# A spectral block with a feed-forward layer: memory laid out anew, a second output set, weight parts dealt out anew, and another order of asking in the planner

## The chip, the cores and the metric

The kernel runs on one core of one Trainium2 chip. The metric is the device time of one execution in microseconds (us); the profiler's views come from one profiled execution of the same program. The engines are TensorE (PE in the views; PEld is its weight load), VectorE (DVE), ScalarE (ACT), GpSimd (POOL) and SyncE (SP), whose queue issues most of the DMAs.

## The reference

One layer of 4096 tokens of 640 features in float32. The shift, scale and gate vectors come from a small modulation product `silu(c) @ w_mod`.

```python
def _A_ref(x, w1, b1, w2, b2):                 # 4096 tokens, NB = 4 blocks of 160 features
    z = rfft over the tokens, split into the 4 blocks -> zr, zi
    hr = relu(zr @ w1[0] - zi @ w1[1] + b1[0]);  hi = relu(zi @ w1[0] + zr @ w1[1] + b1[1])
    or_ = hr @ w2[0] - hi @ w2[1] + b2[0];       oi_ = hi @ w2[0] + hr @ w2[1] + b2[1]
    or_, oi_ = soft shrinkage of both by 0.01
    return irfft(or_ + 1j * oi_)

def _B_ref(x, w_gate, w_up, w_down):
    return (silu(x @ w_gate) * (x @ w_up)) @ w_down     # 640 -> 1728 -> 640

h = layernorm(x) * (1 + ca) + sa
x = x + ga * _A_ref(h, ...)
h = layernorm(x) * (1 + cb) + sb
x = x + gb * _B_ref(h, ...)
return x
```

## The kernel before

A product keeps float32's accuracy by parts: each operand is rounded to a high part of a shorter float32 form (`F32R`), and the rest is its low part; a product is then high by high, high by low and low by high. So every weight and every activation passes two steps before a matmul may read it: a "high" (a copy or a scaling, on ACT or POOL) and a "low" (a subtract, on VectorE or POOL).

**First half (the spectral part).** The token index is split in 128 by 32 for the Fourier transform. Eight tiles `xa0` to `xa7` of x (each 10,240 bytes of a partition) are normalized and transformed; `write_s1` copies each result to the device memory `s1` in several pieces. The frequencies are then worked in eight chunks `ch` of four blocks `b`, in a loop over positions `p = 4 ch + b` whose order is written out by hand (`manual_schedule`): each engine works its instructions in the order in which they stand in the code. At position p stand, in this order: layer one of block p (`stage_l1`, tiles `pl`, `h`, `u`, `r2`); the second transform for later blocks (`stage_b`, tile `pb`; `evac_b` reads it into the parts `z`, ACT first, then VectorE); `tail_low` of block p; layer two of block p - 1 (`stage_l2`, tile `pc`; two groups of eight matmuls, each followed by a VectorE addition of the bias into `tts`, called `tt`); the inverse transform of a block some positions back (`stage_i`, tile `pi`). After the last block of a chunk, `move_x` copies the chunk's two `tt` tiles by eight DMAs into other tiles, `xx`. The tag `tt` has two buffers, so the next chunk's first addition waits until these copies have landed.

Layer two's weights are three pairs: `w2a`, `w2b` and `w2c`, each of 640 features in two halves o = 0 and 1. `prep2` lists the six jobs in the order w2a 0, w2a 1, w2b 0, w2b 1, w2c 0, w2c 1. The kernel before gives POOL the highs of jobs 0, 2 and 5 and the low of 5; ACT has the highs 1, 3 and 4, and VectorE the lows 0 to 4 (0 and 1 ahead of the loop, 2 to 4 at its first position).

The tiles of layer two and of the inverse (pool `p2`) lie in the memory of the `xa` tiles, which is free again when the last copies of a tile have been read. With `reuse_waits="tile"` an instruction that first writes such a tile waits for those older tiles only that lie in the same place. From the addresses: before, `acc`, `cl`, `wx` and `bx` lie in xa0, `w2a` in xa1, `w2b` in xa2, `w2c` in xa3 and the `tt` set in xa4.

**Second half (the feed-forward part).** From about 311 us on, 32 rows of 128 tokens are worked in six tiles, the first two (`plain`) by straight products, the other four (`seven`, `down7`) by seven products of half size for eight. Its order is worked out when the program is built: a planner holds chains of steps, each with an engine, an assumed duration and what it depends on, and keeps an assumed time of each engine. After every stretch of matmuls (`slot`, by 0.3 us) it calls `sweep`, which asks each chain in turn for the steps that may be issued by now. `tails` are short chains that follow a product (the parts of an activation, its products and differences); then come the standing chains, first `gate` (the gate's sum) and `prep` (highs and lows of the gate and up weights, line 1413 on ACT and line 1420 on VectorE). Which step is asked first is issued first on its engine.

Of the kernel before, what the change touches and what calls it, by code (L numbers as in the profile page):

```python
# [6 lines left out]
F32 = mybir.dt.float32  # L7
F32R = mybir.dt.float32r
AF = mybir.ActivationFunctionType
OP = mybir.AluOpType  # L10
# [3 lines left out]
P = 128  # L14
D = 640
# [3 lines left out]
NB = 4  # L19
# [154 lines left out]
def body(tc, x, w1, b1, w2, b2, wg, wu, wd, c, wm, k_fa, k_tb, k_tx, k_bm, k_bx, k_ga, k_ge, k_id, out, dbg=None):  # L174
# [4 lines left out]
    def f32(ap):  # L179
        return ap.bitcast(F32)  # L180
# [21 lines left out]
    with ExitStack() as top:  # L202
# [35 lines left out]
        with ExitStack() as af:  # L238
# [40 lines left out]
            def weights_high(w, h, l, v, sg, eng=None):  # L279
                if eng:  # L280
                    eng.tensor_scalar(w[:, :, h], v, sg, None, op0=OP.mult)
                else:
                    act.activation(w[:, :, h], v, AF.Copy if isinstance(sg, float) else AF.Identity, scale=sg)

            def weights_low(w, h, l, v, sg):
                dve.scalar_tensor_tensor(w[:, :, l], v, sg, f32(w[:, :, h]), op0=OP.mult, op1=OP.subtract)
# [52 lines left out]
            b2t = rp.tile([P, 2, NB, BS], F32, name="b2t")  # L339
            with tc.tile_pool(name="sp", bufs=1) as sp:  # L340
                xas = []

                def load_x(t):
                    xa = xp.tile([P, 4, D], F32, name=f"xa{t}")
                    if t < 3:
                        for i in range(4):
                            nc.sync.dma_start(xa[:, i, :], xv[:, 4 * t + i, :])
                    else:
                        nc.sync.dma_start(xa, xv[:, 4 * t:4 * t + 4, :])
                    xas.append(xa)  # L350
# [156 lines left out]
            nc.sync.dma_start(tx, k_tx)  # L507
            p2 = af.enter_context(tc.tile_pool(name="p2", bufs=1, side="right", reuse_waits="tile"))

            acc = p2.tile([P, D], F32, name="acc")  # L510
            cl = p2.tile([P, D], F32, name="cl")
            wx = p2.tile([P, P], F32, name="wx")
            bx = p2.tile([P, 2, 128], F32, name="bx")
            w2a = p2.tile([P, NB, 640], F32R, name="w2a")
            w2b = p2.tile([P, NB, 640], F32R, name="w2b")
            w2c = p2.tile([P, NB, 640], F32R, name="w2c")
            prep2 = prep_weights(raws[2], w2a, w2b, w2c, False)

            prep2 = [prep2[i] for i in (0, 3, 1, 4, 2, 5)]
            for n in (0, 2, 5):  # L520
                weights_high(*prep2[n], pool)
            w, h, l, v, _ = prep2[5]
            pool.tensor_tensor(w[:, :, l], v, f32(w[:, :, h]), op=OP.subtract)


            nc.sync.dma_start(bx.rearrange("p a b -> p (a b)"), k_bx)
# [55 lines left out]
            pbs = {}  # L582
            rzs = {}
            hss = {}
            tts = {}

            def width(ch):
                return 258 if ch == CE else 256
# [1 line left out]
            def stage_b(ch, t, tag=None):  # L590
                g, tb = gs[ch], tbs[ch]
                pb = (ps.tile([P, 2, 256], F32, tag=tag, name=f"pb{ch}_{t}") if tag else
                      bank0(1 if t == 4 else 0, [P, 2, 256], f"pb{ch}_{t}"))
                col = slice(128 * t, 128 * t + 128)
                for j in range(4):
                    mm(pb[:, :, 64 * j:64 * j + 64], g[:, j, col], tb[:, j, :], start=True, stop=True)
                pbs[ch, t] = pb
# [90 lines left out]
                                         op0=OP.max, op1=OP.subtract)  # L688


            def stage_l2(ch, b, then=()):
                h0, h1, r2, _ = hss[ch, b]
                de = slice(160 * b, 160 * b + 160)
                for q in ((0, 2, 1) if ch == CE else (0, 1)):
                    fs = slice(128 * q, 128 * q + 128) if q < 2 else slice(256, 258)
                    M = 128 if q < 2 else 2
                    W = 320 if q < 2 else 160
                    if b == 0 and q < 2:
                        tts[ch, q] = p2.tile([P, 2, D], F32, tag="tt", bufs=2, name=f"tt{ch}_{q}")
                    pc = ps.tile([P, 512], F32, tag="p2" if q < 2 else "p1", name=f"pc{ch}_{b}_{q}")  # L700
                    seq = [(h0[:, 0, fs], w2a[:, b, 0:W]), (h0[:, 1, fs], w2a[:, b, 0:W]),
                           (h0[:, 0, fs], w2a[:, b, 320:320 + W]),
                           (h1[:, 0, fs], w2b[:, b, 0:W]), (h1[:, 1, fs], w2b[:, b, 0:W]),
                           (h1[:, 0, fs], w2b[:, b, 320:320 + W]),
                           (r2[:, fs], w2c[:, b, 0:W]), (r2[:, fs], w2c[:, b, 320:320 + W])]
                    for i, (l, m) in enumerate(seq):
                        mm(pc[:M, :W], l, m, start=(i == 0), stop=(i == len(seq) - 1))  # L707
                    if q < 2:
                        dve.tensor_tensor(tts[ch, q][:, :, de], pc[:, :320].rearrange("p (r e) -> p r e", r=2),
                                          b2t[:, :, b, :], op=OP.add)  # L710
                        if then:
                            then[q]()
                    else:

                        dve.tensor_tensor(tts[ch, 0][0:1, 1, de], pc[0:1, :160], b2t[0:1, 0, b, :], op=OP.add)
# [52 lines left out]
            e32 = hp.tile([P, 5, 2], F32, name="e32")  # L768
            edge = hp.tile([P, 2, 5, 2, 2], F32R, name="edge")
            zero = hp.tile([P, 2, 5, 2, 2], F32, name="zero")  # L770
            pool.memset(zero, 0.0)
            pool.tensor_copy(edge, zero)


            def edges():
                px = ps.tile([P, 5, 2], F32, tag="p3", name="px")
# [13 lines left out]
                evac_b(0, b)  # L790
                evac_r(0, b)
            weights_high(*prep2[1])
            for job in prep2[0:2]:
                weights_low(*job)


            def shrink_last(q, hf):
# [28 lines left out]
            for p in range(LAST + 1):  # L826
                ch, b = p // 4, p % 4
                on(shrink, p - 6)
                on(stage_l1, p)


                if p < 4:
                    todo = ([(0, 2)], [(0, 3)], [(1, 4), (1, 0)], [(1, 1)])[p]
                elif b == 0:
                    todo = [(ch, 3)]
                else:
                    todo = [(ch + 1, 4)] * (b == 1) + [(ch + 1, b - 1)]
                todo = [q for q in todo if q[0] < NCH]
                for q in todo:
                    stage_b(*q)  # L840
                    if q[1] < 4:
                        evac_b(*q)
                for f, *a in sums.get(p, ()):
                    f(*a)

                rows = [p + 2] * (p < 4) + [p + 3] * (p > 2)
                for k in rows:
                    on(evac_rh, k)
                on(tail_l1, p)
                on(shrink_high, p - 6)  # L850
                for k in rows:
                    on(evac_rl, k)
                on(tail_low, p)
                on(stage_l2, p - 1)
                if p == 3:
                    stage_b(1, 2)
                    evac_b(1, 2)
                on(stage_i, p - 7)
                on(shrink_low, p - 6)
                if p < LAST:  # L860
                    on(shrink_parts, p - 5)
                if b == 0 and ch:
                    for i in range(4):
                        move_x(ch - 1, i)
                if p == 0:
                    for n in (3, 4):
                        weights_high(*prep2[n])
                    for job in prep2[2:5]:
                        weights_low(*job)
                if p == 0:  # L870
                    pool.dma_start(bm.rearrange("p a b c -> p (a b c)"), k_bm)
                if p == 2 or b == 3 and 2 < ch + 2 < NCH:
                    load_g(ch + 2)
                    load_tb(ch + 2)
                for f, *a in mods.get(p, ()):
                    f(*a)
                if p == LAST - 4:
                    cf += [rp.tile([P, 2, D], F32, tag=tag, name=f"cf{tag}") for tag in ("rm", "rr")]
                    load_first_rows(rb + 16, rl, nc.sync)
                elif p == LAST - 1:  # L880
                    load_first_rows(0, rb - 16, nc.sync)
# [163 lines left out]
        with ExitStack() as ff:  # L1045
# [76 lines left out]
            class Chain:  # L1122
# [4 lines left out]
                def add(self, steps):  # L1127
                    for st in steps:
                        if st.key is not None:
                            owner[st.key] = self  # L1130
                    self.steps += steps
# [79 lines left out]

            def sweep():
                held = NT
                for c in tails + chains:
                    if c in tile_of:
                        if tile_of[c] > held:
                            continue
                        tries(c)
                        if c.steps:
                            held = tile_of[c]  # L1220
                    else:
                        tries(c)
                tails[:] = [c for c in tails if c.steps]
# [1293 lines left out]
```

## Time and profile before

| | us |
|---|---|
| runs shown (3) | 1419.41, 1422.27, 1421.2 |
| median | 1421.2 |
| profiled execution, its own time | 1421.44 |
| its span, first to last instruction | 1419.6 |

In a row of the timeline stand the start and the duration in us, the engine, the line, the operation, what is written and read, how many instructions are merged, and in brackets how long the engine was idle before and who ended that. In a row of the waits stand who waited for whom, the sum in us, how often, and the longest. In a row of the stretches stand, for each engine, its busy time in us and its instructions, then the TensorE clock that was granted (1.00 is full), the share of the DMA engines, and GB/s.

### The profile page before, as it was taken

The numbers are of one execution on the slowest core, as the hardware profiler recorded it, in microseconds if no ns is written. First come the engines' busy times: TensorE is split into PE (matmuls) and PEld (weight loads), VectorE is DVE, ScalarE is ACT, GpSimd is POOL, SyncE is SP. The second block draws the span as 40 slices with busy tenths as digits, with TensorE's granted clock in tenths as the row PEclk, the third lists the DMA queues.
The fourth block names the chain that finished last, engine by engine and source line by source line (L and its number), as shares of the span: only waits on it lengthen the run. The fifth ranks groups of instructions, "written<-read, shape, count | busy, mean of one in ns | idle before, by whom it ended". The sixth has DMA issues, their size and how long they took to land.

```text
span 1419.6 us, 23748 instructions
## 1 busy us (share of the span) xinstructions
PE 1386.4 (98%) x8410; PEld 1311.5 (92%) x8410; DVE 1055.8 (74%) x1863; ACT 766.7 (54%) x1542; POOL 599.3 (42%) x681
## 2 busy tenths in 40 slices
PE   6899999999999999999999999999999999999998
PEld 2599999977989899899999999999999999999998
DVE  8979888889888888649786758787678757365654
ACT  6869999756555545546463446446264624252341
POOL 5600210047767765336454535357153524052241
PEclk9999999999999999999999999999999999999999
DMA  9866556666797997899867998788998667965634
GB/s 360 314 235 201 166 170 193 204 224 205 272 369 283 316 339 267 284 372 320 308 207 274 351 342 287 279 296 270 373 319 289 228 219 274 339 209 194 216 118 148
DMA packets 170872, 377.34 MB, mean 266 GB/s; under 512 B 22177, under 2 KB 81633, under 8 KB 168738
## 3 DMA queue, kind: packets, MB, share of 16 engines
q1 hardware_dynamic: 161650, 359.28, 72.9%
q0 software_dynamic: 6800, 13.93, 3.0%
q10 hardware_dynamic: 2304, 2.62, 0.5%
q8 instruction: 66, 1.08, 0.3%
q14 instruction: 52, 0.43, 0.1%
HBM read 269.48 MB, written 96.80 MB: 258 GB/s over the span
## 4 chain that ended last, share of the span: by engine, by line
PE 83%; DVE 5%; ACT 3%; DMA 3%; POOL 2%; issue 2%; SPq 1%; ACTq 0%; DVEq 0%; POOLq 0%
PE pw L2028 9%; PE pw L2030 9%; PE pw L2029 9%; PE pc L2329 8%; PE pd L2245 7%; PE pe L2329 6%; PE pg L1953 4%; PE pg L1952 4%; PE pg L1951 4%; PE pc L707 4%; PE pl L657 3%; PE pw L2041 2%; PE pw L2039 2%; PE pw L2040 2%; PE py L1666 2%
## 5 line engine op out<-in xcount | busy, mean ns | idle before, releaser
L1420 DVE TENSOR_TENSOR wb<-r,wb 128x768 fp32r<-128x768 f32 (+3 forms) x170 | 161.8, 961 | 11.5 <-ACT wb L1413 11.0
L2028 PE MATMUL pw<-h,wt 128*128 128x384 f32 x412 | 139.4, 338 | 1.7 <-ACT s_v L2047 1.4
L2030 PE MATMUL pw<-h,wt 128*128 128x384 f32 x412 | 138.3, 336 | 0.0
L2029 PE MATMUL pw<-h,wt 128*128 128x384 f32 x412 | 138.0, 335 | 0.0
L2108 DVE TENSOR_TENSOR L<-sg,L 128x384 fp32r<-128x384 f32 x144 | 106.8, 762 | 38.0 <-ACT L L2104 37.3
L1413 ACT ACTIVATE wb<-r 128x768 fp32r<-128x768 f32 (+3 forms) x168 | 104.3, 638 | 53.4 <-PE pw L2041 42.7
L2329 PE MATMUL pc<-wq,L 128*128 128x320 f32 x846 | 132.2, 309 | 0.0
L2329 PEld LDWEIGHTS pc<-wq,L 128*128 128x128 f32 x846 | 126.2, 188 | 0.7 <-DVE s_v L2054 0.3
L2088 POOL TENSOR_TENSOR sg<-s_x,sg 128x384 f32<-128x384 f32 x24 | 31.4, 1307 | 218.3 <-DVE s_x L2054 218.3
L2028 PE MATMUL pw<-h,wb 128*128 128x384 f32 x312 | 105.0, 336 | 0.0
L2029 PE MATMUL pw<-h,wb 128*128 128x384 f32 x312 | 104.4, 335 | 0.0
L2030 PE MATMUL pw<-h,wb 128*128 128x384 f32 x312 | 104.3, 334 | 0.0
L2329 PE MATMUL pe<-wq,L 128*128 128x320 f32 x648 | 102.4, 310 | 1.4 <-DMA wq<-wqd 1.4
L1953 PE MATMUL pg<-ht,wb 128*128 128x512 f32 x260 | 101.4, 390 | 1.5 <-DVE wb L1420 1.5
L1951 PE MATMUL pg<-ht,wb 128*128 128x512 f32 x260 | 101.9, 392 | 0.0
L2047 ACT ACTIVATE s_x<-pw 128x384 f32<-128x384 f32 x52 | 25.5, 491 | 140.9 <-PE pw L2030 138.9
L1952 PE MATMUL pg<-ht,wb 128*128 128x512 f32 x260 | 101.3, 390 | 0.0
L2099 POOL TENSOR_TENSOR sg<-sg,sg 128x384 f32<-128x384 f32 x72 | 92.1, 1279 | 17.2 <-DVE L L2108 13.7
L2329 PEld LDWEIGHTS pe<-wq,L 128*128 128x128 f32 x648 | 96.6, 188 | 1.7 <-DVE x L2286 1.7
L2245 PE MATMUL pd<-wq,a 128*128 128x320 f32 x632 | 96.0, 310 | 0.0
L2245 PEld LDWEIGHTS pd<-wq,a 128*128 128x128 f32 x632 | 93.4, 188 | 0.5
L764 POOL DMA_DIRECT2D s<-co x28 | 15.8, 563 | 180.0 <-ACT co L763 176.7
(317 smaller groups left out, 3903.3 us busy)
## 6 DMA issues: line engine op xcount, KB each, us to landing
wq<-wqd SPq DMA_DIRECT2D x83, 640.0 KB, 5.7
wt<-td SPq DMA_DIRECT2D x103, 512.0 KB, 5.2
hs<-ho SPq DMA_DIRECT2D x52, 512.0 KB, 5.9
h<-hs SPq DMA_DIRECT2D x32, 768.0 KB, 7.9
td<-wt SPq DMA_DIRECT2D x25, 512.0 KB, 5.3
r<-in_B_w_gate_dram SPq DMA_DIRECT2D x24, 384.0 KB, 5.2
r<-in_B_w_up_dram SPq DMA_DIRECT2D x24, 384.0 KB, 4.0
xx<-tt SPq DMA_DIRECT2D x56, 160.0 KB, 3.2
```

Source lines behind the costliest of these rows:

```text
L1413: def high(ks, e=slice(0, c), copy=lambda o, i: act.activation(o, i, AF.Copy)):
L1420: dve.tensor_tensor(wbs[t, n][:, 1, ks, e], raw[t, n][:, ks, e], f32(wbs[t, n][:, 0, ks, e]), op=OP.subtract)
L1951: mm(b, wh, hh, start=(kk == 0), stop=False)
L1952: mm(b, wh, hl, start=False, stop=False)
L1953: mm(b, wl, hh, start=False, stop=(kk == 4))
L2028: mm(b, w(0, kp), a[:, kp, 0], start=start and kp == 0, stop=False, skip_group_check=not start)
L2029: mm(b, w(0, kp), a[:, kp, 1], start=False, stop=False, skip_group_check=not start)
L2030: mm(b, w(1, kp), a[:, kp, 0], start=False, stop=kp == 1, skip_group_check=not start)
L2099: pool.tensor_tensor(o, x, y, op=op)
L2108: dve.tensor_tensor(o[:, 1], raws[j], f32(o[:, 0]), op=OP.subtract)
L2245: mm(b[:, :320], l, m, start=start and i == 0, stop=stop and i == len(s) - 1)
L2329: mm(o[:, :320], ls[q][:, x, k], w[:, q, y], start=start and q == 0 and n == 0, stop=q == 1 and n == 2, skip_group_check=not start)
```

## The change

- The `xa` tiles are made in the order 1, 2, 3, 0, 4, 5, 6, 7, and `p2` begins with `w2a`, `w2b`, `w2c`, then `acc`, `cl`, `wx`, `bx`, a tile `gap` that nothing uses, and the new `tu` set. By the sizes, `w2a` then lies below the `xa` tiles in memory that held nothing, `w2b` in xa1's place, `w2c` in xa2's, `acc` to `gap` in xa3's, the `tu` set in xa0's, and the `tt` set, as before, in xa4's.
- Odd chunks write their output to `tu`, even chunks to `tt`.
- POOL has the highs of the weight jobs 0, 2 and 3 and the lows of 1, 3 and 5; ACT the highs of 1, 4 and 5; VectorE the lows of 0, 2 and 4.
- At position 3, layer two's matmuls stand where they stood, but its two additions come behind `evac_b(1, 2)` and `tail_low`.
- `zero` and `edge` are filled after the weights of the first position rather than before the loop.
- `sweep` asks `gate` and `prep` ahead of `tails`.

```diff
@@ first half, ahead of the loop
+                xts = {t: xp.tile([P, 4, D], F32, name=f"xa{t}") for t in (1, 2, 3, 0, 4, 5, 6, 7)}
                 def load_x(t):
-                    xa = xp.tile([P, 4, D], F32, name=f"xa{t}")
+                    xa = xts[t]
...
+            w2a = p2.tile([P, NB, 640], F32R, name="w2a")
+            w2b = p2.tile([P, NB, 640], F32R, name="w2b")
+            w2c = p2.tile([P, NB, 640], F32R, name="w2c")
             acc = p2.tile([P, D], F32, name="acc")
             cl = p2.tile([P, D], F32, name="cl")
             wx = p2.tile([P, P], F32, name="wx")
             bx = p2.tile([P, 2, 128], F32, name="bx")
-            w2a = p2.tile([P, NB, 640], F32R, name="w2a")
-            w2b = p2.tile([P, NB, 640], F32R, name="w2b")
-            w2c = p2.tile([P, NB, 640], F32R, name="w2c")
+            p2.tile([P, 896], F32, name="gap")
+            tts = {(1, q): p2.tile([P, 2, D], F32, tag="tu", bufs=2, name=f"tt1_{q}") for q in range(2)}
...
-            for n in (0, 2, 5):
+            for n in (0, 2):
                 weights_high(*prep2[n], pool)
-            w, h, l, v, _ = prep2[5]
-            pool.tensor_tensor(w[:, :, l], v, f32(w[:, :, h]), op=OP.subtract)
+
+            def weights_rest(n):
+                w, h, l, v, _ = prep2[n]
+                pool.tensor_tensor(w[:, :, l], v, f32(w[:, :, h]), op=OP.subtract)
...
-            def stage_l2(ch, b, then=()):
+            def stage_l2(ch, b, then=(), held=None):
...
-                    if b == 0 and q < 2:
-                        tts[ch, q] = p2.tile([P, 2, D], F32, tag="tt", bufs=2, name=f"tt{ch}_{q}")
+                    if b == 0 and q < 2 and ch != 1:
+                        tts[ch, q] = p2.tile([P, 2, D], F32, tag="tu" if ch % 2 else "tt", bufs=2, name=f"tt{ch}_{q}")
...
-                        dve.tensor_tensor(tts[ch, q][:, :, de], pc[:, :320].rearrange("p (r e) -> p r e", r=2),
-                                          b2t[:, :, b, :], op=OP.add)
+                        add = lambda q=q, pc=pc: dve.tensor_tensor(
+                            tts[ch, q][:, :, de], pc[:, :320].rearrange("p (r e) -> p r e", r=2), b2t[:, :, b, :], op=OP.add)
+                        if held is None:
+                            add()
+                        else:
+                            held.append(add)
...
-            pool.memset(zero, 0.0)
-            pool.tensor_copy(edge, zero)
...
             weights_high(*prep2[1])
-            for job in prep2[0:2]:
-                weights_low(*job)
+            weights_low(*prep2[0])
+            weights_rest(1)
+            weights_high(*prep2[3], pool)
+            weights_rest(3)
@@ first half, in the loop
-                on(tail_low, p)
-                on(stage_l2, p - 1)
                 if p == 3:
+                    adds = []
+                    stage_l2(0, 2, held=adds)
                     stage_b(1, 2)
                     evac_b(1, 2)
+                    on(tail_low, p)
+                    for f in adds:
+                        f()
+                else:
+                    on(tail_low, p)
+                    on(stage_l2, p - 1)
...
                 if p == 0:
-                    for n in (3, 4):
+                    for n in (4, 5):
                         weights_high(*prep2[n])
-                    for job in prep2[2:5]:
-                        weights_low(*job)
-                if p == 0:
+                    weights_rest(5)
+                    for n in (2, 4):
+                        weights_low(*prep2[n])
+                    pool.memset(zero, 0.0)
+                    pool.tensor_copy(edge, zero)
                     pool.dma_start(bm.rearrange("p a b c -> p (a b c)"), k_bm)
@@ second half
             def sweep():
                 held = NT
-                for c in tails + chains:
+                for c in [gate, prep] + tails + chains:
```

More of the change, by code (lines that the diff above doesn't have):

```diff
@@ L584, in body @@
             hss = {}
-            tts = {}
             def width(ch):
```

## The prediction

> **What bounds the kernel.** I read the page first, then busy time by stretches, then who waited for whom on TensorE, and last the timelines around each wait. The profiled execution took 1421.4 us, 1.8 us more than its span; it lies 0.2 us above the median of the runs shown (1421.2), so the sum is made against 1421.4 and carries over. A difference under 0.2% (2.8 us) cannot be told from no change here.
>
> ```profile
> span 1419.6 us, 23748 instructions
> ...
> PE 1386.4 (98%) x8410; PEld 1311.5 (92%) x8410; DVE 1055.8 (74%) x1863; ACT 766.7 (54%) x1542; POOL 599.3 (42%) x681
> ```
> ```profile
> core 0: us, PE busy (x) PEld busy (x) DVE busy (x) ACT busy (x) POOL busy (x), PEclk, DMA share, GB/s
> 60.00:92.00 32.00, 27.77 (x205) 26.86 (x204) 25.34 (x48) 22.62 (x49) 7.07 (x6) 0.95 0.87 321
> 95.00:255.00 160.00, 158.68 (x1235) 156.72 (x1234) 137.27 (x268) 148.78 (x305) 16.78 (x51) 1.00 0.60 188
> ...
> 335.00:600.00 265.00, 263.48 (x1400) 233.23 (x1399) 218.52 (x302) 139.71 (x244) 174.27 (x168) 1.00 0.83 292
> 600.00:1360.00 760.00, 754.63 (x4634) 750.09 (x4633) 516.70 (x916) 342.72 (x732) 318.98 (x331) 1.00 0.81 283
> ```
>
> TensorE bounds it: 98% busy, and the change adds and removes no matmul. So it can win only TensorE's idle time and its slowed time, and lose by new waits. The first half (up to 311 us) has its one poor stretch at 60 to 92 us: 4.2 us idle, at a mean clock of 0.95. From 95 to 255 us 1.3 us are idle, in the second half 1.5 and 5.4 us. TensorE's waits name them:
>
> ```profile
> PE pc L707 <- DVE w2b L286: 2.4, 1, 2.4
> ...
> PE pg L1953 <- DVE wb L1420: 1.5, 1, 1.5
> PE pb L596 <- DVE z L604: 1.5, 2, 1.0
> ...
> PE pe L2329 <- DMA wq<-wqd: 1.4, 1, 1.4
> PE pw L2028 <- ACT s_v L2047: 1.4, 2, 1.1
> ...
> PE pi L760 <- DVE u L675: 1.0, 2, 0.8
> ```
>
> **Layout and weight parts (A).** Layer two's first block stands waiting for its weight parts, and right behind the wait its clock is halved:
>
> ```profile
> 66.26 0.45 PE L707 MATMUL pc<-w2b,h 128*128 128x320 f32 x2
> 69.12 0.41 PE L707 MATMUL pc<-w2b,h 128*128 128x320 f32 x1 [2.41 <-DVE w2b L286]
> ...
> 70.01 0.39 PE L707 MATMUL pc<-w2c,r 128*128 128x320 f32 x1 [0.33 <-DVE w2c L286]
> ...
> 71.73 0.85 PE L657 MATMUL pl<-z,w1a 128*128 128x256 f32 x3
> ...
> 77.12 0.68 PE L707 MATMUL pc<-w2a,h 128*128 128x320 f32 x3
> ```
> ```profile
> 31.00:32.00 1.00, 0.00 (x0) 0.00 (x0) 1.00 (x4) 1.00 (x3) 0.92 (x2) 1.00 0.98 384
> ```
> ```profile
> 71.00:71.50 0.50, 0.50 (x4) 0.50 (x4) 0.50 (x2) 0.42 (x1) 0.00 (x0) 0.50 1.04 412
> ...
> 74.00:74.50 0.50, 0.50 (x5) 0.50 (x4) 0.29 (x1) 0.50 (x2) 0.00 (x0) 0.59 0.97 383
> ```
>
> The clock is 0.50 from 71.0 to about 74.4: 3.4 us at half speed cost 1.7 us. Together with the idle 2.4 and 0.3 us that makes 4.4 us in one place. What the parts wait for:
>
> ```profile
> 56.70 1.91 POOL L281 TENSOR_SCALAR w2a<-rm 128x640 fp32r<-128x640 f32 x1 [4.82 <-PE pb L596]
> ...
> 59.84 0.74 ACT L283 ACTIVATE w2a<-rm 128x640 fp32r<-128x640 f32 x1
> ...
> 60.85 1.56 DVE L286 SCALAR_TENSOR_TENSOR w2a<-rm,w2a 128x640 fp32r<-128x640 f32 x2
> ...
> 61.67 2.41 POOL L281 TENSOR_SCALAR w2b<-rm 128x640 fp32r<-128x640 f32 x1 [3.06 <-DMA s<-xa]
> ...
> 64.17 1.81 POOL L281 TENSOR_SCALAR w2c<-rr 128x640 fp32r<-128x640 f32 x1
> ...
> 65.24 0.81 ACT L283 ACTIVATE w2c<-rr,sgn 128x640 fp32r<-128x640 f32 x1
> ...
> 66.06 1.57 POOL L523 TENSOR_TENSOR w2c<-rr,w2c 128x640 fp32r<-128x640 f32 x1
> ...
> 66.26 2.81 DVE L286 SCALAR_TENSOR_TENSOR w2b<-rm,w2b 128x640 fp32r<-128x640 f32 x2
> ...
> 68.99 0.87 DVE L286 SCALAR_TENSOR_TENSOR w2c<-rr,sgn,w2c 128x640 fp32r<-128x640 f32 x1
> ...
> 73.40 0.89 DVE L709 TENSOR_TENSOR tt<-pc,b2t 128x320 f32<-128x320 f32 x2 [0.23 <-DMA s<-xa]
> ```
>
> POOL stands idle 3.06 us until the copies of `xa` out of w2b's place have landed. In the new layout w2a lies outside the `xa` tiles, w2b in the place of xa1 and w2c in that of xa2; xa1's copies are issued before xa2's, which are what w2b waits for now. So that idle time goes, and POOL takes three highs and three subtracts instead of three and one; VectorE does three subtracts instead of five. Undisturbed: w2b's first high would end near 60.5, the w2a subtract at 62.2 (behind ACT's high of 59.84), w2b's second high at 64.0 and its subtract at 65.6. ACT ends its last w2c high near 66.1, as now, so the last subtract ends near 67.7, and TensorE would go on 2.4 us earlier than 70.0.
>
> But POOL and VectorE disturb one another: two VectorE subtracts take 1.56 us alone and 2.81 beside the 1.57 us of a POOL subtract. Three POOL subtracts now meet VectorE's path. If the first delays VectorE by those 1.25 us, they eat the 0.78 us of the subtract taken from in front of it: VectorE reaches its last two not at 66.26 but near 66.7, and 2.81 more make 69.5, against 69.86 for the last one now. That is the value I take, being the measured neighbour of the same operations: 0.4 us earlier. The clock: in the 3.4 us before 71.0 some 1.5 of the 2.41 us and the 0.33 were idle, and the drop followed; a whole idle microsecond at 31 us brought none. With 0.4 us less idle I take it that the drop goes, 1.7 us; this is the weakest step. A: 2.1 us gained.
>
> The bounds: at worst 0, when z of the next block, which queues behind the same subtract, also delays TensorE by half a microsecond and the clock drops all the same. At best 3.1 us. The addition at 73.40 writes over xa4, whose copies stay in SyncE's queue where they are and end its wait there; the second block needs a bank that this addition frees, near 74.0, and it starts at 77.12 now. This is what comes due next once the weights are early.
>
> [...]
>
> The memset and copy of `zero` and `edge`, and the `bm` load behind them on POOL, now pass behind the last subtract; chunk 4 and the first inverse, their first readers, are whole chunks off: nothing.
>
> **Held additions (B).** At position 3, VectorE takes the last block's rest, two additions, and only then z for the next chunk:
>
> ```profile
> 87.79 0.42 DVE L687 SCALAR_TENSOR_TENSOR r<-u,r 64x256 fp32r<-64x256 f32 x1
> 88.24 0.89 DVE L709 TENSOR_TENSOR tt<-pc,b2t 128x320 f32<-128x320 f32 x2
> 89.05 0.74 DVE L604 SCALAR_TENSOR_TENSOR z<-pb,ca,z 128x512 fp32r<-128x512 f32 x1
> ```
> ```profile
> 89.85 1.16 PE L596 MATMUL pb<-tb,g 128*128 128x128 f32 x8 [1.03 <-DVE z L604]
> ```
>
> Put first, z ends 1.3 us earlier, more than the wait of 1.03. Behind it the rest and the additions end 0.7 us later; who waits for them is the following layer-two block, which comes behind the eight matmuls of the last row (1.16 us). B: 1.0 gained, between 0.3 and 1.0.
>
> **Second output set (C).**
>
> ```profile
> DVE tt L709 <- DMA xx<-tt: 9.5, 6, 2.2
> ```
> ```profile
> 129.53 0.49 DVE L709 TENSOR_TENSOR tt<-pc,b2t 128x320 f32<-128x320 f32 x1 [1.84 <-DMA xx<-tt]
> ```
> ```profile
> 133.69 0.41 PE L760 MATMUL pi<-xh,bm 128*128 128x320 f32 x1 [0.80 <-DVE u L675]
> ```
>
> Six times VectorE waits for the copies out of the single set. With two sets these 9.5 us go, but TensorE feels little of them: the late `u` after them holds back the inverse, 1.0 us in two waits. C: 1.0 gained, between 0.5 and 1.5. The new set lies where the second half's first down weights are loaded, so that load now waits for the last inverse; its first reader needs the gate's sum, which comes later still: nothing.
>
> **Scheduler (D).** Asking `gate` and `prep` before `tails` changes who comes first on ACT and VectorE wherever both are ready; no step is added. One wait is of that kind:
>
> ```profile
> 485.11 1.22 DVE L1988 TENSOR_TENSOR a<-sg,a 128x512 fp32r<-128x512 f32 x1
> ...
> 486.98 0.94 DVE L1420 TENSOR_TENSOR wb<-r,wb 128x768 fp32r<-128x768 f32 x1
> ```
>
> The weight's subtract stands behind a tail's, and TensorE waits 1.5 us. In the new order it comes first and most of that goes. All else after it is dealt anew: the other waits (1.4 on a DMA, 1.4 behind ACT's `s_v`) may vanish or be joined by others. I take 0.5 gained; ends 3.5 gained (nearly half of the 6.9 us idle) and 3 lost (three more waits like the longest `s_v`).
>
> **Sum.** 2.1 + 1.0 + 1.0 + 0.5 = 4.6 us: 1421.4 - 4.6 = 1416.8 us. What is won in the first half reaches the end, as TensorE is the bound after it as well.
>
> **The rivals.** [...] POOL's subtracts block VectorE so far that the stall and the half clock stay: A is 0, the rest 2.5, 1418.9 us. For it: the 2.81. Against it: POOL's lost 3.06 us come back, and VectorE has two subtracts fewer. (2) *The reordered second half gives it back, evenly.* D at 3 lost instead of 0.5 gained: 1420.3. (3) *Slower.* A weight copy put ahead of ACT's `s_v` or `s_y` copies holds a bank that the next product needs, 1.1 us each as in the longest row. The first half's 4.1 us are used up at four such waits; it is measurably slower from seven on, and at eight the time is 1421.4 - 4.1 + 8.8 = 1426.1. For it: such waits exist. Against it: two of that kind in all of the second half now, and the scheduler keeps ACT copies back while a bank is due.
>
> **How the numbers follow.** Forecast 0.62, (1) 0.2, (2) 0.06, (3) 0.12. Faster by over 0.2%: 0.62; within it: 0.26; slower: 0.12. Range: at the low end A 3.1, B 1.0, C 1.5 and D 3.5 make 9.1, 1412.3; at the high end A 0, B 0.3, C 0.5 and D 2 lost make 1.2 slower, 1422.6.
>
> **What would show it.** Right: no POOL wait for `s<-xa` before w2b; TensorE's wait at the first layer-two block under 2.2 us; clock 1.00 from 70 to 75 us; `tt<-pc` no longer waiting for `xx<-tt`; no wait for z near 86 us; no 1.5 us wait for `wb`. Wrong: a half clock still standing, a new wait of TensorE for POOL's w2a or w2b, or over 9 us idle between 335 and 1360 us.

## The result and the profile after

| | before | after |
|---|---|---|
| median, us | 1423.12 (16 executions, 1419.41 to 1428.56) | 1416.28 (16, 1412.37 to 1421.28) |
| ratio | | 0.9955, 95% interval 0.9943 to 0.9967 |
| profiled execution, its own time | 1421.44 | 1416.59 |
| its span | 1419.6 | 1414.8 |

A second set of 12 executions of the changed kernel gave 1417.77 and a ratio of 0.9961 (0.9948 to 0.9974). The change saves about 6 us (6.4 and 5.5 by the two ratios); 4.6 were forecast. The page and the stretches of the changed kernel, in the columns of before:

```profile
span 1414.8 us, 23753 instructions
...
PE 1384.8 (98%) x8410; PEld 1313.1 (93%) x8410; DVE 1073.3 (76%) x1861; ACT 764.7 (54%) x1542; POOL 603.6 (43%) x683
```
```profile
core 0: us, PE busy (x) PEld busy (x) DVE busy (x) ACT busy (x) POOL busy (x), PEclk, DMA share, GB/s
60.00:92.00 32.00, 29.05 (x215) 28.38 (x215) 26.18 (x48) 23.16 (x51) 8.38 (x7) 0.95 0.87 317
95.00:255.00 160.00, 158.41 (x1233) 156.81 (x1233) 137.90 (x268) 149.23 (x306) 16.70 (x51) 1.00 0.61 190
335.00:600.00 265.00, 263.18 (x1403) 233.60 (x1402) 226.15 (x305) 138.87 (x244) 175.70 (x168) 1.00 0.85 295
600.00:1360.00 760.00, 756.81 (x4656) 754.48 (x4655) 528.53 (x917) 343.65 (x736) 323.37 (x334) 1.00 0.81 282
```

From 60 to 92 us TensorE is idle 2.95 us instead of 4.2, but the mean clock is still 0.95. From 95 to 255 us nothing is won (1.6 idle, 1.3 before). From 600 to 1360 us 3.2 are idle instead of 5.4. TensorE's waits from 60 us on:

```profile
PE py L1681 <- DVE chl L1671: 1.9, 1, 1.9
PE py L1681 <- DMA gt<-in_k_ga_dram: 1.8, 1, 1.8
PE pc L711 <- POOL edge L885: 1.7, 1, 1.7
PE pi L768 <- DVE u L679: 1.5, 2, 1.3
PE pw L2054 <- ACT s_z L2062: 1.4, 1, 1.4
...
PE pc L2344 <- DMA wq<-wqd: 1.0, 1, 1.0
PE pb L600 <- DVE z L608: 0.9, 1, 0.9
```

The wait for `wb` is gone, and of the two for z the one near 90 us. In their place stand a wait for the load of `gt` (514 us), for `s_z` (975 us), and more for `u`. The first layer-two block in the timeline:

```profile
64.76 1.16 PE L600 MATMUL pb<-tb,g 128*128 128x128 f32 x8 [0.94 <-DVE z L608]
65.68 0.69 PE L711 MATMUL pc<-w2a,h 128*128 128x320 f32 x3
...
68.40 0.38 PE L711 MATMUL pc<-w2b,h 128*128 128x320 f32 x1 [1.75 <-POOL edge L885]
...
69.20 0.39 PE L711 MATMUL pc<-w2c,r 128*128 128x320 f32 x1 [0.26 <-DVE w2c L286]
...
71.04 0.84 PE L661 MATMUL pl<-z,w1a 128*128 128x256 f32 x3
```
```profile
60.12 1.55 POOL L528 TENSOR_TENSOR w2a<-rm,w2a 128x640 fp32r<-128x640 f32 x1 [0.19 <-ACT w2a L283]
...
65.92 1.65 POOL L528 TENSOR_TENSOR w2c<-rr,w2c 128x640 fp32r<-128x640 f32 x1 [0.28 <-PE pb L600]
```
```profile
60.32 2.03 DVE L286 SCALAR_TENSOR_TENSOR w2a<-rm,w2a 128x640 fp32r<-128x640 f32 x1
...
66.20 2.06 DVE L286 SCALAR_TENSOR_TENSOR w2b<-rm,w2b 128x640 fp32r<-128x640 f32 x1
68.18 0.87 DVE L286 SCALAR_TENSOR_TENSOR w2c<-rr,sgn,w2c 128x640 fp32r<-128x640 f32 x1
...
72.89 0.89 DVE L713 TENSOR_TENSOR tt<-pc,b2t 128x320 f32<-128x320 f32 x2 [0.53 <-DMA s<-xa]
```

The second wait at w2b is 1.75 us instead of 2.41 (the row names POOL's fill of `edge`, which the matmul doesn't read; VectorE's part of w2b, which it reads, ended at 68.26), that at w2c 0.26 instead of 0.33. But z, for which TensorE waits just ahead of this block (64.76), is late by 0.94 instead of 0.46: VectorE's first subtract takes 2.03 us beside POOL's. And the matmuls at 71.04 are as slow as before (0.84 for three): the half clock stands. In VectorE's waits from 60 to 310 us, the 9.5 us for the copies `xx<-tt` have turned into 9.1 us for the rows of the modulation weights, whose loads stand behind these copies in SyncE's queue:

```profile
DVE acc L543 <- DMA wm<-in_w_mod_dram: 6.8, 4, 2.4
...
DVE acc L541 <- DMA wm<-in_w_mod_dram: 2.3, 2, 1.8
```
```profile
119.15 6.28 SPq L731 DMA_DIRECT2D xx<-tt  x8
125.53 5.16 SPq L536 DMA_DIRECT2D wm<-in_w_mod_dram  x2
```
```profile
129.44 0.89 DVE L543 SCALAR_TENSOR_TENSOR acc<-wm,sc,acc 128x640 f32<-128x640 f32 x1 [2.39 <-DMA wm<-in_w_mod_dram]
```

**The half-clock stretches start on a grid.** The rows below, the first three of the changed kernel, the others of the kernel with the first half's change alone, each hold one start (or, the third, the end) of a half-clock stretch: a mean of 0.77 over 1 us at 0.50 or 1.00 puts the start 0.46 us before the row's end.

```profile
69.50:70.50 1.00, 1.00 (x7) 1.00 (x6) 0.97 (x3) 0.26 (x2) 0.00 (x0) 0.77 1.05 413
329.00:330.00 1.00, 1.00 (x7) 0.90 (x6) 1.00 (x3) 0.79 (x2) 0.00 (x0) 0.73 1.01 387
73.00:74.00 1.00, 1.00 (x8) 1.00 (x8) 0.87 (x3) 0.84 (x2) 0.00 (x0) 0.77 1.17 398
```
```profile
68.00:69.00 1.00, 0.55 (x3) 0.35 (x3) 1.00 (x3) 0.96 (x3) 0.70 (x2) 0.83 1.00 392
488.00:489.00 1.00, 1.00 (x4) 0.82 (x5) 0.97 (x2) 1.00 (x3) 1.00 (x1) 0.75 0.40 149
655.00:656.00 1.00, 1.00 (x7) 1.00 (x7) 1.00 (x4) 1.00 (x4) 0.00 (x0) 0.87 0.00 0
```

Starts at 70.04 and 329.46, end at 73.46, so 3.42 us long; starts at 68.66, 488.50 and 655.74. The distances 259.42, 419.84 and 167.24 come nearest to 76, 123 and 49 such lengths, and divided by these numbers they give 3.4134, 3.4133 and 3.4131 us. So in these two profiles the stretches started on a grid of 3.413 us, whose first point lies 1.77 us from the span's start in the one and 0.39 in the other. A wait near 2 us did not always bring half speed: the 1.75 us at w2b stood ahead of a stretch in the changed kernel, while the clock was 1.00 behind 1.76 us with the early loads and 1.8 without the hold (both told below). That enough of the wait has to fall between two grid points is the author's reading. A stretch costs 1.7 us (3.42 us at a clock of 0.50). The mean granted clock of every execution gives an estimate of how many it had: (1 - clock) x span / 1.71, good to 0.4 for one execution, as the clock is on record to 0.001. With that, times can be compared without this lottery (the kernels are named by their edits, told below); over all 208 executions, within kernels, 0.001 of mean clock goes with 1.5 us (1.4 by this count). The 77 of the kernel before are those that ran beside the experiments, in three sets; their mean number of stretches was 1.3, 2.0 and 1.8, their mean without stretches 1420.2, 1420.0 and 1419.8.

| kernel | n | median us | ratio to before, 95% | half-clock stretches | mean us without them, 95% | first part, second part |
|---|---|---|---|---|---|---|
| before | 77 | 1422.8 | | 1.6 | 1420.1 ± 0.3 | 253.8, 1105.2 |
| after | 16 + 12 | 1416.3, 1417.8 | 0.9955, 0.9961 (above) | 1.7 | 1414.2 ± 0.6 | 251.8, 1101.1; 251.3, 1102.6 |
| sweep alone | 11 + 12 | 1421.6, 1424.0 | 0.9999 (0.9988 to 1.0011), 1.0004 (0.999 to 1.0019) | 2.8 | 1417.9 ± 0.7 | 253.9, 1101.7; 255.7, 1101.5 |
| first half alone | 12 | 1422.0 | 1.0002 (0.9988 to 1.0016) | 2.1 | 1418.5 ± 1.0 | 251.5, 1107.7 |
| old dealing | 12 | 1417.7 | 0.9968 (0.9954 to 0.9983) | 1.2 | 1415.8 ± 1.1 | 253.3, 1103.5 |
| one set | 12 | 1417.4 | 0.9967 (0.9954 to 0.998) | 1.0 | 1416.0 ± 0.8 | 253.1, 1103.3 |
| no hold | 12 | 1417.9 | 0.9957 (0.9943 to 0.9972) | 1.5 | 1415.0 ± 1.1 | 253.3, 1101.9 |
| fill | 6 | 1415.6 | 0.9948 (0.9928 to 0.9968) | 0.8 | 1414.5 ± 1.3 | 252.1, 1101.3 |
| early wm | 6 | 1413.6 | 0.9938 (0.9913 to 0.9962) | 1.2 | 1412.4 ± 1.6 | 249.5, 1101.6 |
| prep first | 8 | 1417.8 | 0.9965 (0.9953 to 0.9977) | 1.4 | 1414.8 ± 1.1 | 252.3, 1104.0 |
| fill, early wm | 6 | 1412.7 | 0.9933 (0.9918 to 0.9947) | 0.7 | 1411.8 ± 1.6 | 250.2, 1102.6 |
| the same, early gt | 6 | 1417.0 | 0.996 (0.9946 to 0.9974) | 0.6 | 1415.4 ± 1.7 | 249.5, 1105.4 |

The last column is of the profiled executions alone, with 1.7 us taken off for each stretch in it: from the layer-one matmul that waits for `rz` near 58 us to the transpose that waits 0.47 us near 312 us (58.43 and 311.98 in the changed kernel), and from there to the end of the span. The three profiles with the old first half (before, sweep alone) have 253.8 to 255.7 us in the first part, the four with exactly the changed kernel's (itself twice, first half alone, prep first) 251.3 to 252.3.

### The profile page after: what moved, and what is told of

Same layout as the page of the kernel before. It is cut to its first block, busy times and chain, and to the rows that moved or that the text cites. A ratio compares the mean times of both kernels' runs of the same rounds, so it can differ in the third digit from the quotient of the medians.

```text
span 1414.8 us, 23753 instructions
## 1 busy us (share of the span) xinstructions
PE 1384.8 (98%) x8410; PEld 1313.1 (93%) x8410; DVE 1073.3 (76%) x1861; ACT 764.7 (54%) x1542; POOL 603.6 (43%) x683
## 5 line engine op out<-in xcount | busy, mean ns | idle before, releaser
L1435 DVE TENSOR_TENSOR wb<-r,wb 128x768 fp32r<-128x768 f32 (+3 forms) x170 | 174.7, 1038 | 13.0 <-ACT wb L1428 12.8
L2123 DVE TENSOR_TENSOR L<-sg,L 128x384 fp32r<-128x384 f32 x144 | 100.7, 723 | 26.4 <-ACT L L2119 25.9
```

The source lines that it names most:

```text
L1435: dve.tensor_tensor(wbs[t, n][:, 1, ks, e], raw[t, n][:, ks, e], f32(wbs[t, n][:, 0, ks, e]), op=OP.subtract)
L2123: dve.tensor_tensor(o[:, 1], raws[j], f32(o[:, 0]), op=OP.subtract)
```

## The experiments

**Sweep alone, and the first half alone.** The first is the kernel before with the line of `sweep`, the second the changed kernel without it.

```diff
-                for c in tails + chains:
+                for c in [gate, prep] + tails + chains:
```

> The kernel before, with the planner's new order of asking alone; the first half is untouched. The prediction gives this part 0.5 us (ratio 0.9996). The comparison of the two traces speaks for more: from the start of the feed-forward part's second matmul group to the end, the changed kernel wins 4.0 us, though a half-clock window of 3.4 us fell into it that may come or not. So the trace's theory: 4 us faster (ratio near 0.9972), TensorE idle between 335 and 1360 us at 5 us instead of 6.9, no 1.5 us wait for wb. A rival, that the second half's gain in the traces is noise of the waits: within 1.5 us of before.

> The changed kernel with the planner's old order of asking: all of the first half's changes and nothing else. The prediction gives these 4.1 us (ratio 0.9971): 2.1 for layout and weight parts, 1.0 for the held additions, 1.0 for the second set. The traces say 2 us (ratio 0.9986): about 0.3 for the weights, since the half clock stands in both, 1.2 for the held additions and nothing lasting for the second set. The sum of this run's and the sweep run's gains should be the whole, 6.4 us, if the halves are independent.

Each alone measures as no change (1421.6 and 1422.0 us); together they give about 6 us. Without the half-clock stretches they are worth 2.14 and 1.54 us, together 5.85. Two things are in it. The sweep alone had 2.8 stretches per execution. And with the old sweep, the second half gave back in the profile what the first had won. In the kernel with the first half alone TensorE waits

```profile
PE pg L1968 <- DVE wb L1435: 3.1, 2, 2.6
PE pw L2054 <- ACT s_z L2062: 2.3, 1, 2.3
```

where before it was 1.5 for `wb` and nothing for `s_z`, and its second part took 1107.7 us instead of 1105.2. Why, VectorE's timeline shows for `wb`: it started the subtract at 486.90 us, as before (486.98), though it began the chain of work in front of it at 473.47 rather than 475.41 us:

```profile
473.47 2.56 DVE L1435 TENSOR_TENSOR wb<-r,wb 128x256 fp32r<-128x256 f32 x2 [1.00 <-ACT wb L1428]
...
486.90 0.94 DVE L1435 TENSOR_TENSOR wb<-r,wb 128x768 fp32r<-128x768 f32 x1
```

The same place in the kernel before:

```profile
475.41 3.41 DVE L1420 TENSOR_TENSOR wb<-r,wb 128x256 fp32r<-128x256 f32 x2 [1.68 <-ACT wb L1413]
```

In between, the same instructions took longer in sum (the two pairs of `ho` 2.66 and 1.29 us instead of 1.29 and 0.75, a `wb` 1.22 instead of 0.68). TensorE came earlier and waited longer. This is one profile; that it explains all of the 2.2 us (± 1.4) by which 5.85 exceeds the two isn't shown.

> The kernel before with the new sweep alone, a second time. Its first executions had on average 2.3 half-clock stretches against 1.6 of the kernel before, which at 1.7 us each hide 1.2 us of gain. If these were luck, it now lies 1 to 3 us below the kernel before. If the sweep alone really is worth nothing (its waits of 1.9, 1.7 and 1.4 us bring more half-clock stretches), it comes out the same within 0.1% again. By the profiles alone, without the half-clock stretches, it would be 3.8 us faster.

The sweep alone again: 1424.0 us, 3.0 stretches against 1.8 of the kernel before beside it (2.4 against 1.3 in the first set). So its stretches were no luck of one set. It has three waits near 2 us (2.50 at 68.8, 1.92 at 330.9, 1.85 at 514.6 us), near or above the 1.86 to 2.01 us of idle time that stood ahead of the stretches in the profiles of before and after (last section).

**The old dealing of the weight parts, in the new layout.**

```diff
-            for n in (0, 2):
+            for n in (0, 2, 5):
...
+            weights_rest(5)
...
-            weights_low(*prep2[0])
-            weights_rest(1)
-            weights_high(*prep2[3], pool)
-            weights_rest(3)
+            for job in prep2[0:2]:
+                weights_low(*job)
...
-                    for n in (4, 5):
+                    for n in (3, 4):
...
-                    weights_rest(5)
-                    for n in (2, 4):
-                        weights_low(*prep2[n])
+                    for job in prep2[2:5]:
+                        weights_low(*job)
```

> The changed kernel with the weight parts dealt as before (POOL: three highs and one subtract, VectorE: five subtracts), in the new layout. If POOL's three subtracts are what eats the gain of the layout, TensorE's wait at the first layer-two block ends earlier than in the changed kernel, z of block 2 is no longer late (0.46 instead of 0.94 us), and the kernel is 0.5 to 1 us faster than the changed one. If the new dealing helps as the prediction had it, the wait is longer here by 0.5 us or more and the kernel slower by as much.

1417.7 us; without stretches 1.6 ± 1.3 slower than the changed kernel. With the old dealing the layout cuts the wait for w2b to 1.2 us and leaves z where it was (0.5), so the three waits at the first block make 2.0 us, against 2.95 with the new dealing and 3.2 before: there the new dealing costs 1.0 us, as the first expectation had it. But then the second block waits, and the time is not the better for it:

```profile
75.79 0.71 PE L713 MATMUL pc<-w2a,h 128*128 128x320 f32 x3 [1.47 <-DVE tt L715]
```
```profile
75.25 0.89 DVE L715 TENSOR_TENSOR tt<-pc,b2t 128x320 f32<-128x320 f32 x2 [3.60 <-DMA s<-xa]
```

That is what the prediction named as due next, the addition over xa4. In this execution the copies out of xa4 ended 2.4 us later than in the changed kernel (72.89); why is open.

**One output set,** the second set's memory left empty.

```diff
-            tts = {(1, q): p2.tile([P, 2, D], F32, tag="tu", bufs=2, name=f"tt1_{q}") for q in range(2)}
+            p2.tile([P, 4, D], F32, name="gap2")
+            tts = {}
...
-                    if b == 0 and q < 2 and ch != 1:
-                        tts[ch, q] = p2.tile([P, 2, D], F32, tag="tu" if ch % 2 else "tt", bufs=2, name=f"tt{ch}_{q}")
+                    if b == 0 and q < 2:
+                        tts[ch, q] = p2.tile([P, 2, D], F32, tag="tt", bufs=2, name=f"tt{ch}_{q}")
```

> The changed kernel with one output set for all chunks (the second set's memory is kept empty). The prediction gives the second set 1.0 us, so this would be 1.0 us slower than the changed kernel, with VectorE waiting about 9.5 us for the copies again. The traces' theory: VectorE's wait has only moved to the modulation weights' loads (9.1 us in the changed kernel, not there before), which stand behind the same eight copies in SyncE's queue, so the time stays within 0.5 us of the changed kernel's and the wait for those loads goes while the wait for the copies comes back.

1417.4 us; without stretches 1.8 ± 1.0 slower than the changed kernel, 1.4 in the profiles' first part (253.1 against 251.7, the mean of the four profiles named below the table). So the second set is worth more than the 0.5 us that the second theory of the expectation left it. VectorE waits again for the copies, and TensorE's new wait is not before `u` but at the end of the half, at 290 us, for ScalarE's `co`:

```profile
DVE tt L714 <- DMA xx<-tt: 9.3, 6, 2.0
```
```profile
PE pi L769 <- DVE u L680: 1.1, 2, 0.9
PE pi L822 <- ACT co L772: 0.9, 1, 0.9
```

**The changed kernel again, and three edits of it.**

> The changed kernel once more, as the measure for the three beside it. If the 6.8 us of the first measurement are the change's own, it lies again 5 to 7 us below the kernel before (1415 to 1417.5 us), and its executions at a mean granted clock of 1.000 lie near 1413 us as four of them did then. If the sweep alone and the first half alone are worth nothing together either, and the first measurement was luck, it comes out near 1420 us.

1417.8 us, as the first expectation had it but for 0.3 us.

Dummy matmuls in the wait for w2b:

```diff
                     for i, (l, m) in enumerate(seq):
+                        if (ch, b, q, i) == (0, 0, 0, 5):
+                            idle(5)
```

> The changed kernel with ten dummy matmuls of 128 columns (1.05 us for eight, where such stand already) ahead of the matmul that waits 1.75 us for the low part of w2b; their result is read by nobody, no work of the kernel is left out. If the idle time brings the half clock, the row of the clock at 70 to 74 us shows 1.00 and the kernel is 1.7 us faster than the changed kernel beside it (about 1414.6 us), unless the addition over xa4, as in the kernel with the old dealing, takes 1.0 to 1.5 us of it back as a wait near 75 us; then 0.2 to 0.7 us remain. If the half clock comes from something else, it stands where it is and the time is the same within 0.5 us. In the profile the stall in front of that matmul shrinks to 0.5 us or less either way.

The timeline, and the clock behind it, from 71 to 75 us:

```profile
66.55 1.27 PE L334 MATMUL pz<-ones 128*128 128x128 f32 x10
68.56 0.38 PE L713 MATMUL pc<-w2b,h 128*128 128x320 f32 x1 [0.74 <-POOL edge L887]
```
```profile
71.00:75.00 4.00, 4.00 (x38) 4.00 (x36) 3.56 (x9) 2.06 (x5) 0.00 (x0) 1.00 1.08 382
```

1415.6 us with 0.8 stretches instead of 2.1 in the changed kernel beside it, and without them the same. In none of the three profiles with the dummies is the clock halved near 70 us; in 6 of the other 11 it is. Three profiles alone could be chance; together with the idle time counted over the steps of the grid (last section) they speak for idle time as what brings it. No wait for the additions over xa4 came up.

The modulation weights loaded one position earlier, every second row into a second tile:

```diff
-            p2.tile([P, 896], F32, name="gap")
+            wm2 = p2.tile([P, D], F32, name="wm2")
+            p2.tile([P, 256], F32, name="gap")
...
-                wmts[m, k] = p2.tile([P, D], F32, tag="wm", bufs=1, name=f"wm{m}_{k}")
+                wmts[m, k] = wm2 if k % 2 else p2.tile([P, D], F32, tag="wm", bufs=1, name=f"wm{m}_{k}")
...
-                    mods.setdefault(4 + 6 * i + k, []).append((mod_load, m, k))
+                    mods.setdefault(3 + 6 * i + k, []).append((mod_load, m, k))
```

> The changed kernel with each row of the modulation weights loaded one position earlier, into two buffers by turns (the second in the memory of the unused gap). If VectorE's 9.1 us of waiting for these loads is what took back the gain of the second output set, these waits go, TensorE's two waits for u (0.24 and 1.31 us) with them, and the kernel is 1 to 1.5 us faster than the changed kernel beside it. If VectorE's wait there is idle time that costs nothing, the time is the same within 0.5 us; the u waits then have another cause and stand.

1413.6 us, without stretches 1.8 ± 1.7 faster than the changed kernel. TensorE's waits for `u` are gone, and from 95 to 255 us it is idle for 0.04 us in all:

```profile
95.00:255.00 160.00, 159.96 (x1252) 159.09 (x1251) 142.87 (x276) 152.33 (x313) 17.52 (x52) 1.00 0.60 189
```

The first part is 249.5 us, 2.2 less than the 251.7 above. So VectorE's 9.1 us were what had taken this back; the earlier issue and the second tile aren't told apart. The same stall at w2b (1.76 us) stands in this profile with no half clock behind it.

The additions of position 3 put back:

```diff
-                    adds = []
-                    stage_l2(0, 2, held=adds)
-                    stage_b(1, 2)
-                    evac_b(1, 2)
-                    on(tail_low, p)
-                    for f in adds:
-                        f()
+                    on(tail_low, p)
+                    stage_l2(0, 2)
+                    stage_b(1, 2)
+                    evac_b(1, 2)
```

> The changed kernel with the two additions of position 3 back in front of z. If the held additions are worth what the two traces show, TensorE's wait of about 1.0 us for z near 86 us is back and the kernel is 1.0 to 1.2 us slower than the changed kernel beside it. The rival: the microsecond is given back at the next wait for u anyway, and the time is the same within 0.5 us.

The medians are the same (1417.9 and 1417.8), without stretches it is 0.8 ± 1.3 slower: the times can't settle it. The trace does: TensorE's waits from 60 to 95 us have the second wait for z, 1.0 us at 87, and the first part is 253.3 us against 251.7.

```profile
PE pb L600 <- DVE z L608: 2.0, 2, 1.0
```

**Which asking matters.**

```diff
-                for c in [gate, prep] + tails + chains:
+                for c in [prep] + tails + chains:
```

> The changed kernel, but sweep asks only prep ahead of tails, and gate where it stood. If the gain of the scheduler's part is that weights no longer stand behind tails (the 1.5 us wait for wb), prep alone has it all: the same as the changed kernel within 1 us. If gate's early steps are what matters, or the luck of a new plan, the wait for wb or others of 1 to 2 us stand in it and it lies 1 to 4 us above the changed kernel.

1417.8 us, without stretches 1414.8: `prep` alone has it, to within what can be measured (± 1.3). No wait for `wb` stands in it.

**The two that help, together,** and then with `gt` loaded earlier (`"G": 3.0` for 1.2 in the planner's `AHEAD`).

> The changed kernel with the ten dummy matmuls and the early loads of the modulation weights together. If the two are worth their own amounts (the loads 1.8 us at the same number of half-clock stretches, the dummies one half-clock stretch of 1.7 us less in those executions that have one near 70 us), it lies some 10 to 12 us below the kernel before, near 1412 us. The rival: without the half clock the additions over xa4 become what is late, or the next stall brings the half clock in its place; then it is no faster than the early loads alone (1413.6 us).

> The one before, and the planner may put a load on POOL's queue 3.0 us ahead of its assumed time rather than 1.2. If the wait of 1.5 to 3.7 us near 512 us comes from the load of gt being put behind POOL's other steps, it goes, and with it the half-clock stretch that follows it in some executions: 2 to 3 us faster than the one before. The rival: the plan behind it is dealt anew by this, as by the change itself, and other waits of the same size come up; then between 2 us faster and 5 us slower.

The first has the lowest median, 1412.7 us, 3.6 and 5.1 us below the two of the changed kernel (3 and 4 by the ratios); that it beats the early loads alone (1413.6) isn't shown. The second took the wait for `gt` away (3.3 us in the profile of the first) and lost, 3.6 ± 2.3 us without stretches: among TensorE's waits from 335 to 1360 us stand new ones, and the second part takes 1105.4 us rather than 1102.6. The rival had it.

```profile
PE pw L2046 <- ACT s_v L2065: 1.7, 2, 1.2
PE pt L1747 <- ACT h L1751: 1.1, 1, 1.1
PE py L1684 <- DVE chl L1674: 1.1, 1, 1.1
PE py L1684 <- ACT chh L1671: 0.9, 1, 0.9
```

## Why the prediction was right or wrong

The time was right, 1416.8 against 1416.3 and 1417.8, but two terms were mis-sized, in opposite directions, and that 1.9 us too many and 2.6 too few nearly cancel is luck. The first half as a whole brought 1.5 ± 1.1 us without stretches and 2.1 in the profiles (253.8 to 251.7), where 4.1 were forecast.

**A, 2.1: too large by almost 1.9.** What it said of the engines held. POOL no longer waits for the copies of `xa`. The shorter stall, 0.4 us, came out as 0.25: 0.73 less at w2b and w2c, 0.48 more at z, which the lower bound had named. The step that failed is "With 0.4 us less idle I take it that the drop goes, 1.7 us", marked as the weakest. The drop stands in the changed kernel's two profiles and not in others with the same stall (1.76 us with the early loads, 1.8 without the hold); on average the kernel has as many half-clock stretches as before (1.7 and 1.6). How much of the stall falls into one step of the grid is set by the grid's place: the step ahead of the drop held 1.86 us of idle time before and 2.01 in the changed kernel, though the stall was shorter. The row at 31 us was no measure either: that step held 1.81 us in the profile of before, and no drop came. The first rival had this part right, and its reason, POOL's subtracts in VectorE's way, too: with the old dealing the three waits of the first block are 1.0 us shorter. Its price of 1418.9 was too high mainly because D was larger. The traces show the delay: in the changed kernel one VectorE subtract took 2.03 and 2.06 us beside a POOL subtract of 1.55 and 1.65, where before two took 1.56 (at 60.85 us) with no POOL subtract beside them.

**B, 1.0: right by the traces.** The wait of 1.03 us near 90 us is gone, and comes back when the edit is undone; the times (0.8 ± 1.3) can't confirm its size.

**C, 1.0: right in size, by another way.** The prediction had the gain in the waits for `u`. These were 1.0 us before and 1.5 and 0.8 in the changed kernel's two profiles. Undoing the second set costs 1.4 to 1.8 us, 0.9 of it in the one profile at the end of the half. What the prediction missed is that VectorE's wait is only handed on, from the output copies to the weight rows queued behind them; without that, 2.2 us more in the profile.

**D, 0.5: too small by some 2.6.** The second part is 3.1 us shorter than before (1102.1, the mean over the ten profiles with the new sweep as the change has it, against 1105.2 in the one of before), near the end of 3.5 that the prediction kept; without stretches the sweep is worth 2.1 ± 0.8 us with the old first half and 4.3 ± 1.2 with the new one. The wait for `wb` went as said. Waits are only part of it: in the second part TensorE was idle 8.8 us before and 7.4 on the mean of the ten; the other 1.7 us lie in its busy time for the same 6463 matmuls (1092.8 and 1091.1 us, slowed time taken off), and no run shows what brings them. What was not seen is that the wait for `wb` is also where, in the profile of the first half alone, time won earlier was lost, so that "what is won in the first half reaches the end" would not have held there without D.

Of the signs named: the POOL wait, the stall under 2.2 us, `tt` not waiting for `xx`, no wait near 86 us and no 1.5 us for `wb` all came; the clock of 1.00 from 70 to 75 us did not, and of the signs against it the half clock still standing came. The idle time from 335 to 1360 us is 5.0 us, far from the 9 that would have spoken against it. The slower rival, ScalarE's copies held up by weight copies, shows two such waits (`s_z`, 1.4, and `s_y`, 0.6), not eight. The range's high end takes 2 us lost for D, where D's own end was 3; it made no difference.

Open: why the sweep alone has a stretch more than the changed kernel, whose second half has the same waits; and how much of a second half's time is the luck of its plan. The early `gt` shows that a small edit there moves it by 3 us. To the first, an estimate: if the grid is laid at every place over the idle time of a profile from 35 us on, and a step with 1.74 us or more, the least counted ahead of a stretch, is taken to bring one, the changed kernel's two profiles give 1.6 each, near its 1.7, but those of the sweep alone 1.2 and 1.9, below its 2.8.

## What to carry to other kernels

Before costing a stall that sits beside a slowed clock, count the slowed stretches in several executions: the mean granted clock of each run gives an estimate, and here it goes with over half (0.58) of the variance within kernels. When a queue's wait goes, read what stands behind it in the same queue, for that may inherit the wait (here 9.5 us for the copies became 9.1 for the loads behind them). And a gain upstream counts only as far as no later wait is set by another engine's own pace (with the first half alone the waits for `wb` were 3.1 us instead of 1.5); so parts that each measure as nothing may be worth 6 us together, as these were.

## What was not expected of the hardware

The half-clock stretches lasted 3.40 to 3.42 us: 3.41 from 71.00 us in the profile of before, 3.42 and 3.41 from 70.04 and 329.46 in the changed kernel, 3.40, 3.40 and 3.42 with the first half alone. In the last two profiles the starts lie whole multiples of 3.413 us apart, on grids 1.77 and 0.39 us from the span's start. The step of this length ahead of a stretch held 1.86 us of TensorE's idle time before, 2.01 and 1.94 in the changed kernel. By the author's count over all profiles that had such stretches (from the first matmul to 1400 us) it held 1.74 to 3.41 us; no stretch followed a step with less, and six steps with 1.81 to 1.90 us (all but one near 30 us; there 1.81 both before and in the changed kernel) brought none. Nor did the 8.0 us in which TensorE was idle ahead of its first matmul: behind them the clock was 1.00 before and in the changed kernel. So idle time of 1.74 us or more in a step stood ahead of every stretch, but what else it takes is not shown. In the second profile of the sweep alone, by the same count, the 2.50 us wait at 68.8 us was cut by a grid point, 1.5 us of idle time on either side, and no half clock came. The load of `gt`, by one instruction in the same place, made TensorE wait 1.8 us in one execution of the changed kernel and 3.7 in the other:

```profile
PE py L1681 <- DMA gt<-in_k_ga_dram: 3.7, 1, 3.7
```
